# A decode kernel with w4 loaded in four pieces of 17, 7, 3 and 1 rows, and the last projection ahead of the w4 sums

## The chip, the cores and the metric

The kernel runs on one core of one Trainium2 chip. The metric is device time in microseconds (us) of one execution, as the median of several runs. Every run told here is marked fast in the record, that is, undisturbed. The profile is one of those runs, taken by the hardware profiler; the span it shows (400.9 us before the change) is some 1.8 us shorter than the device time of the same run. Times such as "at 389.4" count from the start of the span of the profile in question.

## The reference, cut to what matters

One token goes through attention over a long cache and through a small mixer with an MLP, and the two are added:

```python
def _A_ref(x, k_cache, v_cache, wq, wo):        # 32 query heads, 4 key heads, 65536 keys of 128
    ...
    p = _softmax(scores, axis=-1)
    o = jnp.einsum("bhqk,bhkd->bhqd", p, v)
    return (...)(o, ...).reshape(B, Sq, Hq * Dh) @ wo          # wo: 4096 x 1024

def _B_ref(x, w1, w2, w3, w4):
    ...
    h2 = _gelu(_layernorm(x1, axis=-1) @ w3) @ w4               # w4: 3584 x 1024
    return x1 + h2

xn = _layernorm(x, axis=-1)
return x + _A_ref(xn, ...) + _B_ref(xn, ...)
```

Caches and weights together are 170 MB of bf16 that have to be read once, for one token. That is nearly all the work there is.

## The kernel before

The loads form one stream through three large buffers. All are issued on one queue: wq, w3, w1 and w2, then K and V blocks in turn. At the end come the last K block, wo, the last V block, and w4. The 3584 rows of w4 lie as 28 per partition ("rows" below means these 28), and they are loaded in pieces so that the matmuls can start before the last has landed:

```python
W4_PIECES = (6, 5, 6, 4, 3, 2, 1, 1)
...
elif it == "w4":
    w4_v = B_w4.rearrange("(m c) n -> m c n", c=FC)             # FC = 28
    c0 = 0
    for n in W4_PIECES:
        go(out=t[:, c0 * D:(c0 + n) * D], in_=w4_v[:, c0:c0 + n, :].rearrange("p c n -> p (c n)"))
        c0 += n
```

All that is added into the result goes into one accumulator, `psB`. Its two halves of 512 columns use two column groups of the tensor engine, so two matmuls of one column each run side by side:

```python
def row_acc(j, lhsT, rhs, start=False):
    nc.tensor.matmul(psB[32 * j:32 * j + lhsT.shape[1], :], lhsT=lhsT, rhs=rhs, start=start, stop=False,
                     tile_position=(0, 32 * j), skip_group_check=True)
```

The end of the kernel:

```python
compute_k(NU - 1)
tail["rows"] = ps_S.tile([P, SUBS, 512], F32, name="o_acc", tag="sc")
for g in range(HKV - 1):
    project(g)                      # 48 matmuls with wo for three head groups, while the last V block lands
add_projection()                    # VectorE copies that row; four one-row fp32 additions into psB
compute_v(NU - 1)                   # 64 matmuls with V, then VectorE's chain and one matmul (pm_e) make the last oT
early = sum(W4_PIECES[:2])          # 11 rows
compute_w4(0, early)                # 22 matmuls
project(HKV - 1)                    # 16 matmuls, need the last oT
compute_w4(early, FC)               # 34 matmuls

out_t = ogpool.tile([64, 512], BF16, name="out_t", tag="og")
nc.scalar.copy(out=out_t[:], in_=psB[0:64, :])
...
```

A scheduler places the instructions of each engine. In the compiled program the additions of `add_projection` stand behind the V matmuls (the code issues two, and the trace counts four fp32 instructions; likewise it counts two for the one fp32 `pm_e`), and the sums' matmul (`pm_e`, line L391) stands in the middle of the 22 early w4 matmuls.

## Time and profile before

| | before |
|---|---|
| device time, median (3 runs) | 402.85 us (402.81 to 403.03) |
| profiled span | 400.9 us |
| load queue, share of 16 DMA engines | 98.4% |
| tensor engine busy | 57% of the span |
| last V load seen by the tensor engine | 379.90 us |
| last w4 piece seen | 397.32 us |
| last matmul ends | 397.76 us |

The queue part of the profile page before the change (packets, MB, share of the DMA engines' time):

```profile
q1 hardware_dynamic: 4560, 169.87, 98.4%
q8 instruction: 8, 0.13, 0.1%
```

The engines that load are never free, so the kernel is bound by its loads. Only what happens between the last loads and the end of the program can be changed.

The end of the chain of waits before the change (start us, length us, what):

```profile
332.09 6.57 PE oacc L370 x48
338.66 0.02 issue
338.68 41.23 DMA big<-in_A_v_cache_dram
379.90 0.02 issue
379.92 17.40 DMA big<-in_B_w_dram
397.32 0.04 issue
397.36 0.40 PE psB L179 x2
397.76 0.02 issue
397.78 0.58 ACT out_t L443
```

Read from the bottom: the cast waits for the last two matmuls, these for the last w4 row, and before them there is nothing but loading. The tensor engine's own work is nowhere in the last 58 us but for those 0.40 us.

The timeline of the end before the change (start us, length us, engine, line, operation, output<-inputs, number, and in brackets the idle time ahead and what ended it):

```profile
380.39 3.67 PE L370 MATMUL oacc<-big,p_sb 128*32 128x512 bf16 x58
...
385.39 1.02 PE L179 MATMUL psB<-o_rows,ident_f 1*1 1x512 f32 x4 [1.33 <-DVE o_rows L415]
...
386.34 1.24 PE L179 MATMUL psB<-big,hT 128*1 128x512 bf16 x10
...
387.85 0.49 PE L391 MATMUL pm_e<-ol,sel8big 128*128 128x129 f32 x2 [0.26 <-DVE ol L390]
...
388.27 1.46 PE L179 MATMUL psB<-big,hT 128*1 128x512 bf16 x12
...
389.12 0.23 DVE L400 TENSOR_SCALAR oT<-o,rl 128x8 bf16<-128x8 f32 x1
...
389.56 1.89 PE L179 MATMUL psB<-big,oT 128*1 128x512 bf16 x16
...
394.81 0.81 PE L179 MATMUL psB<-big,hT 128*1 128x512 bf16 x6 [0.87 <-DMA big<-in_B_w_dram]
```

While VectorE makes the last oT (until 389.35), the tensor engine does 22 w4 matmuls of the pieces that have landed by then. Afterwards it waits for the loads, 1.7 us in all.

The granted clock in the windows in which the trace reports it, 3.41 us long (stretch, its length, busy time and number for each engine, then the granted clock as a share, the DMA share, GB/s):

```profile
382.38:385.79 3.41, 2.08 (x28) 0.69 (x22) 1.67 (x2) 0.00 (x0) 0.00 (x0) 1.00 1.00 416
385.79:389.20 3.41, 3.15 (x26) 1.06 (x24) 2.73 (x7) 0.00 (x0) 0.00 (x0) 1.00 1.00 421
389.20:392.62 3.42, 3.42 (x34) 1.32 (x31) 0.15 (x1) 0.00 (x0) 0.00 (x0) 1.00 1.00 413
```

### The profile page before, as it was taken

The numbers are of one execution on the slowest core, as the hardware profiler recorded it, in microseconds if no ns is written. First come the engines' busy times: TensorE is split into PE (matmuls) and PEld (weight loads), VectorE is DVE, ScalarE is ACT, GpSimd is POOL, SyncE is SP. The second block draws the span as 40 slices with busy tenths as digits, with TensorE's granted clock in tenths as the row PEclk, the third lists the DMA queues.
The fourth block names the chain that finished last, engine by engine and source line by source line (L and its number), as shares of the span: only waits on it lengthen the run. The fifth ranks groups of instructions, "written<-read, shape, count | busy, mean of one in ns | idle before, by whom it ended". The sixth has DMA issues, their size and how long they took to land.

```text
span 400.9 us, 2563 instructions
## 1 busy us (share of the span) xinstructions
PE 230.4 (57%) x1348; PEld 44.2 (11%) x854; DVE 209.0 (52%) x154; ACT 27.3 (7%) x35; POOL 5.3 (1%) x28
## 2 busy tenths in 40 slices
PE   0470970591668246922965195629453936594985
PEld 0210000010200110010102010201020002000231
DVE  0511010974196549644953894269349931975040
ACT  1001010003000200020002000100100020002000
POOL 2000000000000000000000000000000000000000
PEclk9995795597679666968796799568866986697999
DMA  9989999999999999999999999999999999999895
GB/s 412 425 366 433 451 425 425 503 425 418 414 419 432 418 497 420 425 418 425 432 433 471 425 425 418 433 432 432 464 420 425 418 445 394 428 481 432 380 418 205
DMA packets 4575, 170.01 MB, mean 424 GB/s; under 512 B 467, under 2 KB 469, under 8 KB 982
## 3 DMA queue, kind: packets, MB, share of 16 engines
q1 hardware_dynamic: 4560, 169.87, 98.4%
q8 instruction: 8, 0.13, 0.1%
q14 instruction: 1, 0.01, 0.0%
q10 hardware_dynamic: 6, 0.00, 0.0%
HBM read 169.87 MB, written 0.00 MB: 424 GB/s over the span
## 4 chain that ended last, share of the span: by engine, by line
DMA 52%; DVE 26%; PE 16%; ACT 3%; another core or an unknown queue 2%; issue 1%; DVEq 0%; ACTq 0%
DMA big<-in_A_k_cache_dram 31%; DVE big L315 19%; DMA big<-in_A_v_cache_dram 10%; PE sc L320 8%; PE oacc L370 6%; DMA big<-in_A_wq_dram 6%; DMA big<-in_B_w_dram 4%; DVE p_sb L341 3%; DVE mx L325 3%; ACT p_sb L338 3%; PE psq L245 1%; PE pm_mx L327 0%; DVE m L329 0%; PE pm_mx L334 0%
## 5 line engine op out<-in xcount | busy, mean ns | idle before, releaser
L320 PE MATMUL sc<-big,qdiag 128*128 128x512 bf16 x512 | 127.7, 409 | 66.4 <-DVE big L315 66.4
L315 DVE STREAM_TRANSPOSE big<-big 128x4096 f32<-128x4096 f32 x32 | 139.4, 4413 | 50.5 <-DMA big<-in_A_k_cache_dram 50.4
L370 PE MATMUL oacc<-big,p_sb 128*32 128x512 bf16 x512 | 44.7, 521 | 34.5 <-DVE p_sb L341 34.5
L325 DVE TENSOR_REDUCE mx<-sc 128x1 f32<-128x2048 f32 x8 | 18.3, 2292 | 29.8 <-PE sc L320 29.8
L320 PEld LDWEIGHTS <-qdiag 128*128 128x128 bf16 x128 | 13.0, 102 | 176.6 <-issue 145.9
L338 ACT ACTIVATE p_sb<-sc,nball 128x2048 bf16<-128x2048 f32 x8 | 15.7, 1967 | 218.7 <-DVE nball L336 218.7
L341 DVE STREAM_TRANSPOSE p_sb<-p_sb 128x2048 bf16<-128x2048 bf16 x8 | 18.5, 2311 | 18.0 <-ACT p_sb L338 18.0
L370 PEld LDWEIGHTS <-p_sb 128*32 128x32 bf16 x512 | 16.6, 126 | 59.4 <-DVE p_sb L341 35.1
L245 PE MATMUL psh<-big,ln_rep_b 128*32 128x512 bf16 (+1 forms) x64 | 12.4, 941 | 8.0 <-DMA big<-in_B_w_dram 8.0
L409 PE MATMUL o_acc<-big,oT 128*1 128x512 bf16 x48 | 12.5, 428 | 2.4 <-ACT p_sb L338 2.4
L327 PE MATMUL pm_mx<-ident_f,mx 128*1 128x128 f32 x8 | 2.3, 283 | 19.1 <-DVE mx L325 19.1
L284 DVE STREAM_TRANSPOSE h_row<-h_row 128x896 bf16<-128x896 bf16 x1 | 1.1, 1111 | 21.1 <-ACT h_row L283 21.1
L379 DVE SCALAR_TENSOR_TENSOR og<-oacc,wb,og 128x512 f32<-128x512 f32 x4 | 3.0, 745 | 15.7 <-PE oacc L370 15.7
L179 PE MATMUL psB<-big,hT 128*1 128x512 bf16 x56 | 7.4, 378 | 1.8 <-DMA big<-in_B_w_dram 1.7
L193 PE MATMUL pm_ln<-ln_rowsum_a,ones_f 128*128 128x1 f32 x2 | 0.6, 347 | 13.3 <-DVE ln_rowsum_a L191 13.3
L415 DVE COPY o_rows<-o_acc 1x1024 f32<-1x1024 f32 x1 | 1.2, 1212 | 13.3 <-PE oacc L370 13.3
L184 DVE STREAM_TRANSPOSE x_t<-x_row 32x256 bf16<-32x256 bf16 x4 | 2.5, 616 | 8.9 <-DMA x_row<-in_A_x_dram 8.9
L269 POOL COPY qdiag<-qx 32x32 bf16<-32x32 bf16 x16 | 3.2, 203 | 279.9 <-PE sc L320 249.7
L391 PE MATMUL pm_e<-ol,sel8big 128*128 128x129 f32 x8 | 2.3, 370 | 8.2 <-DVE ol L390 8.2
L245 PE MATMUL psq<-big,ln_rep_a 128*32 128x512 bf16 x64 | 5.9, 547 | 1.3 <-DMA big<-in_A_wq_dram 1.3
L257 DVE CAST q_row<-psq 128x512 bf16<-128x512 f32 x1 | 0.7, 691 | 7.9 <-PE psq L245 7.9
L334 PE MATMUL pm_mx<-ident_f,rep 1*128 1x1 f32 x8 | 1.9, 241 | 5.0 <-DVE rep L331 5.0
(95 smaller groups left out, 72.6 us busy)
## 6 DMA issues: line engine op xcount, KB each, us to landing
big<-in_A_wo_dram SPq DMA_DIRECT2D x1, 8192.0 KB, 36.7
big<-in_B_w_dram SPq DMA_DIRECT2D x1, 7168.0 KB, 38.5
big<-in_B_w_dram SPq DMA_DIRECT2D x2, 2048.0 KB, 46.4
big<-in_B_w_dram SPq DMA_DIRECT2D x2, 1536.0 KB, 27.3
big<-in_B_w_dram SPq DMA_DIRECT2D x1, 1280.0 KB, 24.1
big<-in_B_w_dram SPq DMA_DIRECT2D x1, 1024.0 KB
big<-in_B_w_dram SPq DMA_DIRECT2D x1, 768.0 KB, 30.8
big<-in_B_w_dram SPq DMA_DIRECT2D x1, 512.0 KB, 31.5
```

Source lines behind the costliest of these rows:

```text
L179: nc.tensor.matmul(psB[32 * j:32 * j + lhsT.shape[1], :], lhsT=lhsT, rhs=rhs, start=start, stop=False, tile_position=(0, 32 * j), skip_gro ...
L184: nc.vector.transpose(out=x_t[32 * a:32 * a + 32].rearrange("p c j -> p (c j)"), in_=x_row[:, 256 * a:256 * (a + 1)].rearrange("p (i c) -> ...
L245: nc.tensor.matmul(acc[32 * q:32 * q + 32, i, 0:n], lhsT=rep[:, c, :], rhs=cols(c, i, q), start=(c == 0), stop=(c == DC - 1), tile_positio ...
L269: nc.gpsimd.tensor_copy(out=qdiag[at, LEAD:].rearrange("p (x c) -> p x c", x=4)[:, :, 32 * a:32 * a + 8], in_=qx[at, :, 8 * g:8 * g + 8])
L315: nc.vector.transpose(out=words, in_=words)
L320: nc.tensor.matmul(sc[:, e, :], lhsT=qdiag[:, c0:c0 + P], rhs=cols[:, s, e, :, b2, :, r], start=(s == 0 and b2 == 0 and r == 0), stop=(s = ...
L325: nc.vector.reduce_max(out=mx[:], in_=sc[:].rearrange("p e n -> p (e n)"), axis=AX.X)
L338: nc.scalar.activation(out=p_sb[:], in_=sc[:], func=ACTF.Exp, bias=nball[:, b:b + 1], scale=SCALE, accum_out=group["lall"][:, b:b + 1])
L341: nc.vector.transpose(out=flat, in_=flat)
L370: nc.tensor.matmul(oacc[32 * q:32 * (q + 1), :], lhsT=pT[:, e, 32 * t:32 * (t + 1)], rhs=vt[:, :, e, t, :], start=(e == 0 and t < 4), stop ...
L379: nc.vector.scalar_tensor_tensor(out=og[:], in0=oacc[:], scalar=wb[:, 1:2], in1=og[:], op0=ALU.mult, op1=ALU.add)
L409: nc.tensor.matmul(tail["rows"][0:1, h2, :], lhsT=oT[g][:, j:j + 1], rhs=wt[:, g, j, 512 * h2:512 * (h2 + 1)], start=(g == 0 and j == 0), ...
```

## The change

The intent is to load w4 in fewer, larger pieces, and to put the last projection, which depends on the longest chain, ahead of all w4 sums.

```diff
-W4_PIECES = (6, 5, 6, 4, 3, 2, 1, 1)
+W4_PIECES = (17, 7, 3, 1)
...
-    early = sum(W4_PIECES[:2])
+    early = 0
     compute_w4(0, early)
     project(HKV - 1)
     compute_w4(early, FC)
```

Four DMA issues are gone, and the 22 early w4 matmuls stand behind the 16 of the projection.

## The prediction

> **What bounds the kernel now.** It is bound by its load stream. The page shows the DMA engines at 98.4% of the span on the load queue, 424 GB/s, with no idle slice. So only the end matters. The chain that ended last, in order of time, closes with: the last V load landing at 379.90 us, 17.40 us of w4 loads (to 397.32), the last two matmuls (397.36, 0.40 us), the cast (0.58 us), the output store. The tensor engine waits there for w4 four times, 1.7 us in total (the waits of this stretch): it is nearly level with the loads, but behind none.
>
> **Cost of the change.**
> 1. Loads. A row packet of 2,048 bytes takes 84 ns in the trace, one of 12,288 bytes 462, one of 65,536 bytes 2,420: about 9 ns plus size at 27.2 bytes/ns. Each DMA engine carries 8 such packets per piece, so four pieces fewer save 4 x 8 x about 9 ns, near 0.3 us. Estimated landings on the old time axis: 17 rows at 390.2, 7 at 394.5, 3 at 396.4, 1 at 397.05 (was 397.32).
> 2. Order on the tensor engine. Today 22 w4 matmuls run at 386.3 to 387.6 and 388.3 to 389.7, while VectorE makes the last head sums (oT ready at 389.35). Afterwards those 22 come behind the 16 projection matmuls. VectorE's chain and the sums' own matmul (387.85) start no earlier: the sums' matmul already began 0.05 us after its input. So from 389.4 on, 72 matmuls are left. At full clock two column groups overlap and one comes every 0.107 us (16 took 1.73 us before the next group began): 7.7 us, to about 397.1. That alone would just keep pace with the shorter loads, and the end would come 0.2 to 0.3 us earlier.
> 3. Clock. Between 384.06 and 389.4 the engine would now be busy only 1.5 us (four small additions 1.02, the sums' matmul 0.49). In the stretches of 3.41 us in which the trace grants the clock, those with 1.4 us busy or less at full clock were nearly always followed by 0.5 (0.55 us in 361.9 to 365.3, then 0.53 mean clock in 365 to 370); those with 1.6 or more kept 1.00. Before, this stretch had 2.08 and 3.15 us and stayed at 1.00. This agrees with the Trainium skill, "TensorE: Matmul & The Clock Gate", Part 1: the window is 3413 ns, free-running, and an idle one halves the clock. So I expect 0.5 for one window, starting anywhere from 387 to 390.4. Projection matmuls in it take twice as long; 1.2 to 3.4 us of work at half clock costs 0.6 to 1.7 us, by window phase.
>
> **On the critical path.** The -0.3 us of the loads is there only if the tensor engine keeps up. With the half clock it becomes the limiter of the last 8 us: end 397.4 + 0.6 to 1.7, against 397.76 before. Net +0.3 to +1.4 us, at best -0.3, at worst (two cold windows) +2.
>
> **Prediction.** 403.6 us, 8 in 10 within 402.5 to 404.8. Faster by over 2%: 0.01; within 2%: 0.98; slower: 0.01. The tail is some 2% of the span; no mechanism here can move 8 us.
>
> **What would show it.** DMA landings at the four times above; no w4 matmul before 389.4; granted clock 0.5 somewhere in 387 to 394; w4's first matmul starting at 391.1 (full clock) or up to 392.8 (half) without waiting for its load; in the last 5 us no wait, or only short ones, of the tensor engine for w4.
>
> **What would make it wrong.** If the small additions count as enough activity, the clock stays at 1.00 and the time is 402.5. If the 34-KB packets are served less evenly over the DMA engines, the last landing moves by up to 1 us.

## The result

| | before | after |
|---|---|---|
| device time, median (4 runs each) | 402.86 us (402.81 to 403.03) | 403.96 us (403.82 to 404.08) |
| ratio, with its 95% interval | | 1.0028 (1.0014 to 1.0042) |
| last V packet to last w4 packet, from the packet records | 17.42 us | 17.15 us |
| the 16 projection matmuls | 1.89 us | 3.30 us |
| last matmul ends (time axis of each profile) | 397.76 us | 398.68 us |

A ratio is the mean time of one kernel's fast runs over that of the other's of the same rounds, so it is not quite the ratio of the medians. The change cost about 1.1 us. By the threshold of 2% that is "same", but it is clear of the noise.

The end of the chain of waits after the change:

```profile
387.76 0.50 PE pm_e L391 x2
...
389.03 0.24 DVE oT L400
389.27 0.04 issue
389.32 9.37 PE psB L179 x72
398.68 0.02 issue
398.71 0.58 ACT out_t L443
```

The w4 loads are gone from the chain. In their place stand 72 matmuls in one run, from the moment oT is ready. The tensor engine has become the limiter of the end.

The timeline after the change:

```profile
380.21 3.78 PE L370 MATMUL oacc<-big,p_sb 128*32 128x512 bf16 x61
...
385.32 1.02 PE L179 MATMUL psB<-o_rows,ident_f 1*1 1x512 f32 x4 [1.33 <-DVE o_rows L415]
...
387.76 0.49 PE L391 MATMUL pm_e<-ol,sel8big 128*128 128x129 f32 x2 [1.42 <-DVE ol L390]
...
389.32 3.30 PE L179 MATMUL psB<-big,oT 128*1 128x512 bf16 x16 [1.07 <-DVE oT L400]
...
392.45 6.21 PE L179 MATMUL psB<-big,hT 128*1 128x512 bf16 x56
```

The gap of 1.33 us was there before. Gaps of 1.42 and 1.07 us now stand where w4 matmuls used to be, and the same 16 projection matmuls take 3.30 us and not 1.89. The 56 w4 matmuls follow without a single wait for a load. The windows show why the 16 were slow:

```profile
381.97:385.38 3.41, 2.08 (x36) 1.09 (x30) 1.32 (x2) 0.00 (x0) 0.00 (x0) 1.00 0.91 383
385.38:388.79 3.41, 1.45 (x6) 0.33 (x6) 2.76 (x6) 0.00 (x0) 0.00 (x0) 1.00 1.04 447
388.79:392.21 3.42, 2.89 (x14) 0.88 (x16) 0.43 (x2) 0.00 (x0) 0.00 (x0) 0.50 0.89 377
```

In 385.38 to 388.79 the tensor engine was busy for only 1.45 us, and in the next window it was granted half its clock. That agrees with the Trainium skill, "TensorE: Matmul & The Clock Gate", Part 1: windows of 3413 ns, free-running, and half clock after an idle one. What "idle" means for a window that is partly busy, the page does not say, and it turned out to be the interesting part.

### The profile page after: what moved, and what is told of

Its sections match the earlier page's. It is cut to its first block, busy times and chain, and to the rows that moved or that the text cites. A ratio compares the mean times of both kernels' runs of the same rounds, so it can differ in the third digit from the quotient of the medians.

```text
span 402.0 us, 2559 instructions
## 1 busy us (share of the span) xinstructions
PE 234.3 (58%) x1348; PEld 45.7 (11%) x854; DVE 208.9 (52%) x154; ACT 27.3 (7%) x35; POOL 5.4 (1%) x28
## 4 chain that ended last, share of the span: by engine, by line
DMA 47%; PE 24%; DVE 22%; ACT 3%; another core or an unknown queue 2%; issue 1%; DVEq 0%; ACTq 0%
DMA big<-in_A_k_cache_dram 42%; DVE big L315 15%; PE sc L320 11%; DMA big<-in_A_wq_dram 5%; PE oacc L370 5%; PE o_acc L409 3%; DVE mx L325 3%; ACT p_sb L338 3%; PE psB L179 2%; DVE p_sb L341 2%; PE psq L245 1%; PE pm_mx L327 0%; DVE m L329 0%; PE pm_mx L334 0%
## 5 line engine op out<-in xcount | busy, mean ns | idle before, releaser
L320 PE MATMUL sc<-big,qdiag 128*128 128x512 bf16 x512 | 129.9, 415 | 63.2 <-DVE big L315 57.7
L370 PE MATMUL oacc<-big,p_sb 128*32 128x512 bf16 x512 | 46.0, 535 | 34.5 <-DVE p_sb L341 34.5
L370 PEld LDWEIGHTS <-p_sb 128*32 128x32 bf16 x512 | 17.6, 129 | 59.7 <-DVE p_sb L341 35.1
L179 PE MATMUL psB<-big,hT 128*1 128x512 bf16 x56 | 6.2, 379 | 0.0
L376 ACT COPY og<-oacc 128x512 f32<-128x512 f32 x4 | 2.3, 586 | 34.1 <-PE oacc L370 34.1
```

Source lines behind the costliest of these rows:

```text
L320: nc.tensor.matmul(sc[:, e, :], lhsT=qdiag[:, c0:c0 + P], rhs=cols[:, s, e, :, b2, :, r], start=(s == 0 and b2 == 0 and r == 0), stop=(s = ...
L370: nc.tensor.matmul(oacc[32 * q:32 * (q + 1), :], lhsT=pT[:, e, 32 * t:32 * (t + 1)], rhs=vt[:, :, e, t, :], start=(e == 0 and t < 4), stop ...
```

## The experiments

Theory A: the idle stretch earns a half-clock window, and with no work done ahead, its cost reaches the end. Rival B: 72 matmuls after oT are too much even at full clock. Rival C: the 17-row piece lands too late. All kernels gave correct results. The "fillers" below are useless matmuls into a part of `psB` that nothing reads, placed where the tensor engine would be idle. The four kernels of each group ran on one chip and share the runs of the kernel before there: 402.89 us median (11 runs), 402.83 (11), and 402.77 (9).

### First group: parts of the change, and a filled gap

**order_only**: the old pieces with the new order.

```diff
-    early = sum(W4_PIECES[:2])
+    early = 0
```

> The eight old pieces, only the order changed (projection ahead of all 56 w4 matmuls). Theory A (idle tensor engine, half clock for one window, then 72 matmuls with nothing in reserve): still 1.0 to 1.3 us above before, 403.8 to 404.2, granted clock 0.5 in one window between 387 and 394, no wait for w4 before the last pieces. Rival B (the moved work itself, at full clock, is too much for the time left): also about +1.1. Rival C (the late landing of the 17-row piece holds the tensor engine up): back at before, 402.9.

Measured: 403.78 us (403.38 to 405.44, 6 runs), ratio 1.0032 (1.0019 to 1.0044), at the lower end of what theory A expected; its half-clock window lay at 388.49 to 391.90. Its timeline, once oT is ready, is that of the changed kernel:

```profile
389.12 3.25 PE L179 MATMUL psB<-big,oT 128*1 128x512 bf16 x16 [1.07 <-DVE oT L400]
...
392.20 6.21 PE L179 MATMUL psB<-big,hT 128*1 128x512 bf16 x56
```

With the small early pieces all there, the loss is the same. Rival C falls: the order alone makes the loss.

**pieces_only**: the new pieces, with 11 rows still ahead of the projection.

```diff
 # to the changed kernel
-    early = 0
+    early = 11
```

> The four new pieces, with 11 rows still ahead of the projection. The first 22 w4 matmuls must now wait for the 17-row piece, seen by the engine at about 390.2, with the projection behind them. A: idle from 386.4 to 390.2 but for the sums' matmul, a half-clock window, all 72 matmuls start 0.9 us later than in the changed kernel: +1.7 to +2.3 us above before, 404.6 to 405.2. B: 72 matmuls from 390.2 at full clock, 7.7 us: end 397.9 plus 0.2, +0.4 us, 403.3. C: same as A, so this run parts A and B only.

Measured: 405.79 us (404.93 to 406.17, 5 runs), ratio 1.0068 (1.0056 to 1.0080). This is worse than expected. The first w4 matmul waits for the 17-row piece until 390.37, as expected, but the trace has two half-clock windows (386.82 to 393.64), not one, and the 22 matmuls take 4.14 us. Rival B had 403.3 and falls here. The two halves of the change belong together: with the large first piece, the old order is the worst of all.

**warm_after**: the changed kernel with six fillers ahead of the sums' matmul.

```diff
+    def keep_warm(n):
+        for k in range(n):
+            row_acc(2, hT[:, 0:1], st.tiles["wo"][:, 512 * k:512 * (k + 1)], start=True)
...
+        if g == HKV - 1:
+            keep_warm(6)
         nc.tensor.matmul(pe[:, 0:DH + 1], lhsT=sel8big[:], rhs=ol[:], start=True, stop=True)
```

> The changed kernel plus six useless matmuls of 512 columns into an unread part of the accumulator, in the tensor engine's idle time just ahead of the sums' matmul. A: the clock stays at 1.00 from 372 to the end, the 16 projection matmuls take 1.7 us and not 3.1, and the time falls by 1.2 to 1.5 us, to 402.4 to 402.8, that is 0.1 to 0.4 us under before. B and C: it stays at 403.9 or rises, because work was added and none taken away.

Measured: 402.87, 404.61, 402.85, 404.62, 402.58 and 402.64 us. That is two groups: four runs level with the kernel before, two runs worse than the changed kernel. The profiled run was one of the good ones (402.87). Its window with the fillers:

```profile
386.24:389.65 3.41, 2.41 (x12) 0.38 (x3) 2.72 (x7) 0.00 (x0) 0.00 (x0) 1.00 0.87 373
```

And the projection in its timeline:

```profile
389.75 1.89 PE L179 MATMUL psB<-big,oT 128*1 128x512 bf16 x16 [1.07 <-DVE oT L407]
```

The window with the fillers is busy for 2.41 us, the clock stays at 1.00 to the last matmul, and the 16 projection matmuls take 1.89 us again. With work added, the four good runs are about 1.1 us or more below the changed kernel's median (403.96), which B cannot explain. Theory A had expected 402.4 to 402.8 for all, and only two runs lie there. The two slow runs were not explained by the theory as it stood.

**placebo**: the same six fillers, but beside the projection of the third head group, at 374 to 380, where the tensor engine is busy anyway.

```diff
+                if g == HKV - 2 and 3 <= j < 6:
+                    row_acc(2, hT[:, 0:1], wt[:, 0, j, 512 * h2:512 * (h2 + 1)], start=True)
```

> The changed kernel plus the same six useless matmuls, but among the projection matmuls of the third head group at 374 to 380, where the tensor engine is busy anyway and they run beside others in another column group. A: the idle stretch and the half clock stay, time 403.8 to 404.1 as in the changed kernel. If it is faster too, the six matmuls act by something else than by filling the idle stretch.

Measured: 404.32 us (403.46 to 405.55, 6 runs), ratio 1.0038 (1.0024 to 1.0053). The fillers do nothing there, and the trace has its half-clock window at 388.37 to 391.79. The place matters, not the six instructions. Its median is a little above the expected range because its spread is wide.

### Second group: where do the slow runs come from?

The new guess (A2) was that the earlier gap, at 362 to 368, also earns a half-clock window, and that the two together make the slow runs.

**warm_both**: warm_after, and 18 fillers in the earlier gap. **warm_front**: only those 18, in the changed kernel. **both_old_pieces**: as warm_both with the eight old pieces.

```diff
+        if u == NU - 1:                       # behind the last K matmuls
+            for k in range(10):
+                row_acc(2, hT[:, 0:1], cols[:, SETS - 1, k % SUBS, :, 1, :, 1], start=True)
         st.done(("K", u))
...
         nc.vector.tensor_copy(out=nball[:, b:b + 1], in_=pm[:, P:P + 1])
+        if u == NU - 1:
+            for k in range(8):
+                nc.tensor.matmul(psB[64:65, 0:P], lhsT=nball[:, b:b + 1], rhs=ident_f[:], start=True, ...)
```

> The six useless matmuls in the late gap and 18 more in the gap of 362 to 368, ahead of the projection of the first three head groups. Theory A2 (two idle stretches can each cost a half-clock window, and where in time the windows fall decides how much of the second reaches the end): clock 1.00 from 362 on, the 48 projection matmuls end before the last V load lands, no run in the slow group of 404.6 that two of six runs of warm_after were in; all runs 402.4 to 402.8, 0.1 to 0.4 us under before. If the 404.6 group has another cause, it shows up here as well.

> Only the 18 in the early gap. A2: the late gap still earns one half-clock window, so 0.3 to 1.5 us above before (403.2 to 404.4), with the spread of the window's phase, and no run above 404.5 (order_only and placebo had runs at 405.3 to 405.6). If the early gap alone were the cause, this run would be at 402.5 to 402.8.

> The eight old pieces and the new order, with both gaps filled. With the clock at 1.00 the end hangs on the loads, as before: 402.8 to 403.0, and 0.2 to 0.35 us over warm_both, which is the worth of the four pieces less. If warm_both and this are the same, the pieces are worth nothing and the tensor engine alone sets the end.

Measured: warm_both 404.04 us (403.59 to 404.42, 5 runs), warm_front 404.59 (403.39 to 405.00, 6 runs), both_old_pieces 404.24 (404.07 to 404.64, 5 runs). The fillers did their work early on: the clock is at 1.00 from 362 to 386. But all three expectations were missed: warm_both and both_old_pieces are slower than the range given, and so is the median of warm_front, with three of its six runs above 404.5 (404.75 and twice 405.00). A2 falls as the explanation of the slow runs. The windows of warm_both show what was missed:

```profile
382.61:386.02 3.41, 2.10 (x28) 0.57 (x20) 2.05 (x3) 0.00 (x0) 0.00 (x0) 1.00 1.07 459
386.02:389.44 3.42, 3.42 (x10) 0.58 (x3) 1.54 (x2) 0.00 (x0) 0.00 (x0) 0.50 0.85 363
```

The late fillers and the sums' matmul in its timeline:

```profile
386.23 2.72 PE L179 MATMUL psB<-big,hT 128*1 128x512 bf16 x6
...
388.88 0.74 PE L405 MATMUL pm_e<-ol,sel8big 128*128 128x129 f32 x2
```

The window at 382.61 was busy for 2.10 us, and the clock was halved all the same. The kernel before had 2.08 us in the window at 382.38 and kept it. The difference lies in what the engine was busy with. The V matmuls end at 383.89 here, so they fill 1.28 us of the window, and most of the rest is the four additions that contract a single row (`1*1 1x512 f32`). In the kernel before, V runs to 384.06, which is 1.68 us of its window. Over all traces, five windows that were over 1.51 us busy at full clock were followed by half clock. All five are of this kind: 2.08 to 2.10 us, made up of the end of the V matmuls and most or all of the one-row additions (in both_old_pieces also of the first fillers). All other full-clock windows with 1.54 us or more kept the clock, all with 1.38 us or less lost it, and in between both occur. Leave out the one-row additions, and the border is sharp by the busy times of the traces: of the 883 full-clock windows of all 14 traces, every one with 1.40 us or less of matmuls that contract 128 rows lost the clock, and every one with more than 1.41 us kept it (1.402 kept it, 1.403 lost it). The data type is not the reason: the window of warm_both at 365.54 was busy for 2.32 us, 2.12 us of it with fp32 matmuls that contract 128 rows and make one row of output (the early fillers), and kept the clock. So the one-row additions hardly count as activity. And once the window is half-clock, the fillers do harm: they take 2.72 us, the sums' matmul behind them starts at 388.88 and not near 387.6, and oT comes later.

This makes it a matter of where the windows fall. In the traces, the last border between windows before the end of the V matmuls lay anywhere between 381.04 and 383.68. If it falls late, V's end and the first filler are in two windows, and one is too idle. This would give warm_after its two groups of runs, but no slow run of it was profiled, so for those two runs it is argued and not shown.

**mend**: the old order, with pieces that make 11 early rows land just in time, and three pieces less than before.

```diff
 # to the kernel before
-W4_PIECES = (6, 5, 6, 4, 3, 2, 1, 1)
+W4_PIECES = (11, 7, 6, 3, 1)
-    early = sum(W4_PIECES[:2])
+    early = W4_PIECES[0]
```

> The old order with pieces of 11, 7, 6, 3 and 1 rows: 11 rows land at about 386.6, when the tensor engine gets free for them, so the 22 early matmuls both do useful work and keep the clock at 1.00; three pieces less than before save about 0.2 us of loading. 402.6 to 402.8, every run within 0.3 us of the others.

Measured: 402.90 us (402.78 to 403.00, 5 runs), ratio 1.0001 (0.9990 to 1.0013). It is no faster than before, and above the expected 402.6 to 402.8. The loads did get 0.2 us shorter (17.22 us from the last V packet to the last w4 packet), and the time does not show it. But its profiled run happened to show more than was asked for. Its windows:

```profile
383.53:386.94 3.41, 2.08 (x19) 0.44 (x14) 2.12 (x3) 0.00 (x0) 0.00 (x0) 1.00 0.96 401
386.94:390.36 3.42, 3.42 (x17) 1.09 (x17) 1.76 (x4) 0.00 (x0) 0.00 (x0) 0.50 0.99 421
```

The end of its timeline:

```profile
396.60 1.03 PE L179 MATMUL psB<-big,hT 128*1 128x512 bf16 x8 [0.26 <-DMA big<-in_B_w_dram]
```

This run had a half-clock window in the same stretch as the changed kernel, and took 402.78 us. The early matmuls do not keep the clock up for certain. What they give for certain is a reserve: work is done ahead of the projection, so the tensor engine still reaches the last rows before they land, and waits for them (0.26 us) in spite of the slow window.

### Third group: the gap closed, a smaller reserve, and the changed kernel again

**warm_full** and **full_old_pieces**: warm_both and both_old_pieces, with five more fillers right behind the V matmuls (ahead of the one-row additions), seven and not six ahead of the sums' matmul, and two behind it.

```diff
+        if u == NU - 1:
+            for k in range(5):
+                row_acc(2, hT[:, 0:1], vt[:, :, SUBS - 1, k, :], start=True)
+            add_projection()                  # moved here, so that the fillers stand ahead of it
         st.done(("V", u))
...
-            keep_warm(6)
+            keep_warm(7)
...
+        if g == HKV - 1:
+            for k in range(2):
+                nc.tensor.matmul(psB[64:65, 0:P], lhsT=ident_f[:, 0:1], rhs=msk[:]..., start=True, ...)
```

> The changed kernel with every gap from 362 to the last projection filled: 18 useless matmuls early, five between the end of the V matmuls and the four one-row additions, seven before the sums' matmul, two after it. Theory A3: the one-row additions do not count as activity, so warm_both still had a gap of 2.3 us (V's end to the first filler) that made a half-clock window in most of its runs, and the fillers then ran at half speed and held up the sums. With the gap closed: clock 1.00 from 362 to the end, all runs 402.4 to 402.8. Rival D (the order itself is too late by more than the clock, for example because the fillers or the projection run slower than counted): 403.5 or more again, with the clock at 1.00.

> The same fillers with the eight old pieces. A3: the end then hangs on the loads as in before, 402.7 to 403.0; the difference to warm_full is the worth of four pieces less, 0.1 to 0.3 us. If both are equal, either the pieces are worth nothing or the tensor engine sets the end in both, which the last waits for w4 will tell.

Measured: warm_full 404.07 us (403.88 to 404.25, 5 runs), full_old_pieces 404.33 (403.96 to 404.45, 5 runs), both well above what A3 expected. By the time alone this looks like rival D. The trace of warm_full says otherwise. Its windows:

```profile
386.46:389.87 3.41, 2.94 (x20) 0.87 (x16) 1.93 (x5) 0.00 (x0) 0.00 (x0) 1.00 0.92 394
389.87:393.28 3.41, 3.41 (x36) 1.35 (x34) 0.00 (x0) 0.00 (x0) 0.00 (x0) 1.00 0.99 420
```

The end of its timeline:

```profile
389.16 1.89 PE L179 MATMUL psB<-big,oT 128*1 128x512 bf16 x16
390.88 5.51 PE L179 MATMUL psB<-big,hT 128*1 128x512 bf16 x48
397.92 1.03 PE L179 MATMUL psB<-big,hT 128*1 128x512 bf16 x8 [1.52 <-DMA big<-in_B_w_dram]
```

The clock held, the projection took 1.89 us, and 24 of 28 rows were done by 396.39. Then the tensor engine waited 1.52 us for a load. So the order is not too late at full clock, and D falls as the explanation. What was late is the w4 load. The queue part of the profile for the stretch from 394 to 398 us of warm_full names the cause:

```profile
q1 hardware_dynamic: 233, 0.70, 44.4%
q8 instruction: 1, 0.02, 1.7%
```

A fetch of instructions (16,384 bytes, started at 394.94, took 1.11 us by the packet records) shared a DMA engine with the last w4 packets, one of which (6,144 bytes) took 654 ns in place of 236. By 396.75 all other row packets had landed; the last eleven came one after another until 398.09, so one DMA engine alone was behind. In full_old_pieces the last sixteen came in this way, from 396.85 to 398.13. The last w4 packet came 18.49 us after the last V packet, and 18.70 us in full_old_pieces (fetch at 394.63). The twelve other traces have 17.14 to 17.54 us. In them the fetch near the end lies at 383 to 385, or at 396.6 to 396.8 (in warm_both, warm_front and both_old_pieces), when at most six row packets are still to start. Those at 383 to 385 also held a packet up (in the changed kernel one of 34,816 bytes took 1,786 ns, where the median is 1,291), but made no last landing late; why not is not shown. The five kernels with 18 or more fillers have nine such fetches in their traces, and all others have eight. So the likely reading is that the fillers lengthened the program, and one more block of instructions was fetched at the worst moment. The Trainium skill tells both halves of this: "Runtime: NRT & Kernel Launch", section "Instruction fetch mechanics", has engines refill their instructions in 16 KiB blocks through a DMA queue, "mostly hidden", and "DMA: Bandwidth & Descriptors", section "Queues, rings and completion order", has each DMA engine take packets from its queues in turn. The sizes agree. Here, by these records, the fetch was not hidden: the last landing came some 1.3 us late. Whose instructions they were, the records do not say.

So these two runs settle that a full clock removes the delay of the projection, and leave open what the kernel would have taken without that fetch. An estimate from these numbers: the last w4 packet 1.35 us earlier (18.49 less 17.14) would put warm_full near 402.7 us, level with before. It was not tried. The worth of the pieces in time (0.26 us between the medians of the two) cannot be told from runs disturbed like this.

**early6**: the kernel before, with 6 rows ahead of the projection and not 11.

```diff
 # to the kernel before
-    early = sum(W4_PIECES[:2])
+    early = W4_PIECES[0]
```

> The eight old pieces, six rows (12 matmuls) ahead of the projection instead of 11 rows or none. Theory S (what the early matmuls give is mainly a reserve: work done before the projection that a half-clock window can then eat without harm): 60 matmuls are left at 389.3, 6.4 us at full clock and 7.4 to 8.1 with a half-clock window, against 8.0 to the last landing: 402.8 to 403.3, near before. If only a full-clock stretch helped (12 matmuls, 1.3 us, just short of what keeps the clock), it would be at 403.5 or more like order_only (403.78).

Measured: 402.83 us (402.70 to 402.96, 5 runs), ratio 1.0001 (0.9988 to 1.0013). A reserve of 12 matmuls is as good as 22. The profiled run kept the clock at 1.00, so this run alone does not part reserve from clock. All five runs lie within 0.26 us of each other, though, where order_only and after_again, which have no early rows, spread over 2.06 and 1.55 us.

**after_again**: the changed kernel once more, no edit.

> The changed kernel again, for its spread beside these on one chip. The half-clock window's place is a matter of chance from run to run, so not the 0.3 us spread of its first four runs but 403.2 to 405.5 as order_only and placebo had; median 403.6 to 404.4. If the spread is 0.3 us again, chance of place does not explain the spread of the others.

Measured: 404.26 us (403.49 to 405.04, 5 runs), ratio 1.0036 (1.0024 to 1.0049). The small spread of its first four runs was luck. The profiled run was the slowest (405.04), and its windows show one part of why:

```profile
383.49:386.90 3.41, 2.08 (x19) 0.42 (x14) 2.14 (x3) 0.00 (x0) 0.00 (x0) 1.00 0.93 393
386.90:390.32 3.42, 0.94 (x6) 0.53 (x6) 2.38 (x6) 0.00 (x0) 0.00 (x0) 0.50 0.90 384
390.32:393.73 3.41, 3.41 (x18) 1.04 (x20) 0.00 (x0) 0.00 (x0) 0.00 (x0) 0.50 0.99 419
```

There were two half-clock windows in a row. The first was so idle (0.94 us) that a second followed. Its last matmul ended at 399.93, 1.25 us later than in the first profile of the same kernel (398.68, 403.82 us), and its time is 1.22 us longer. Another part was lost before these windows. The earlier half-clock stretch lay at 366.42 to 373.25 here and at 364.90 to 371.73 in the first profile, so more of the 48 projection matmuls of the first three head groups ran slowly: they took 12.99 us and not 12.15, and ended at 381.21 and not 380.54, and the V matmuls behind them at 384.66 and not 384.00. That is 0.67 of the 1.25 us. Between these two profiles, then, the place of the windows explains the difference; that it makes the spread of all the runs is likely, but not shown.

## Why the prediction was right

- **What bounds the kernel: right.** The loads set the end before the change, with the tensor engine nearly level.
- **The loads: right, and without effect.** A saving near 0.3 us was predicted; the stretch from the last V packet to the last w4 packet went from 17.42 to 17.15 us. Counted from the last V load, the four pieces landed within 0.02 us of the four landings that it gave (10.31, 14.61, 16.49 and 17.14 us, where it had 10.30, 14.60, 16.50 and 17.15). None of it reached the time, because the tensor engine had become the limiter, as the prediction said it would with a half clock.
- **72 matmuls at 0.107 us: right.** At full clock warm_full did the first 64 of them in 7.23 us, from 389.16 to 396.39. Taking off 0.38 us for the length of the last one leaves 0.109 us for each.
- **The half-clock window: right in place and size for the first profile.** It came at 388.79 to 392.21, and the projection took 1.41 us more than before. A loss of 0.6 to 1.7 us was predicted. With two windows, as in after_again, the loss is larger. The prediction had this only as the worst case (+2), but it is not rare: after_again, warm_front, both_old_pieces and pieces_only all show it in their one profile. One run of after_again (405.04) lies above the stated range.
- **Where the reasoning was wrong, though the number was not.** The prediction counted the four small additions as 1.02 us of activity and said that windows with 1.6 us or more keep the clock. Five windows with 2.08 to 2.10 us lost it, and the one-row additions were in all of them. It also read the kernel before as one that keeps its clock by the early matmuls. The mend run shows the half-clock window with 22 early matmuls in place, and no loss of time. The early matmuls protect by being done early; keeping the clock is the lesser and less certain part.

## What to carry to other kernels

When a kernel is bound by its loads, work that can be done ahead of a dependent step is a reserve against slow spells of the engine; moving it behind that step takes the reserve away, even if the sum of the work still fits at full clock. In these traces a window was followed by half clock when no more than about 1.40 of its 3.41 us went to matmuls that contract 128 rows; matmuls that contract one row did not prevent it. Filling gaps with useless matmuls is no safe remedy: at half clock they delay what stands behind them, and in a longer program an instruction fetch can fall on the last loads.

## What the Trainium skill lacked or had wrong

- "TensorE: Matmul & The Clock Gate" tells of idle and busy windows, but names no share of a window that has to be busy. In these traces, a window of 3.41 us at full clock with more than 1.41 us of matmuls that contract 128 rows kept the clock, and with 1.40 us or less lost it (883 windows in 14 traces).
- The same page, in its table on why this matters for kernels, advises against idle gaps of the tensor engine over about 3 us. Shorter gaps were enough here: in warm_both the V matmuls end at 383.89 and the first filler starts at 386.23, so the gap is 2.34 us even with the one-row additions in it counted as idle, and the clock was halved.
- The page does not say that matmuls contracting a single row hardly count as activity. Five windows that were 2.08 to 2.10 us busy, up to 1.0 us of it with such fp32 additions, were followed by half clock.
- "Runtime: NRT & Kernel Launch" calls the cost of crossing an instruction block mostly hidden. In two kernels here, a 16,384-byte fetch among the last w4 packets put the last landing off by about 1.3 us (18.49 and 18.70 us after the last V packet, where the others have 17.14 to 17.54).
